# Part of x transposed by the DMA crossbar, and another order of the first half batch, in a fused Sinkhorn attention and bilinear feed-forward kernel

## The chip, the cores and the metric

The kernel runs on one core of a Trainium2 chip. The metric is the device time of one execution in microseconds. Before the change, three runs took 266.49 to 268.1 us, median 268.03 us. A profile is one execution of its own, with a span that leaves out what lies around the program.

## The reference, cut to what matters

Four batches of eight heads, sequence 768 in eight blocks of 96, head dimension 64. Each head has an 8 x 8 matrix P, made doubly stochastic by five Sinkhorn iterations; P mixes the blocks of k and v, and attention runs inside each block. The attention's output, as x of 3072 x 512, goes through a bilinear feed-forward.

```
P = sort_net
for _ in range(5):
    P = exp(P - max(P, -1)); P = P / (sum(P, -1) + 1e-9); P = P / (sum(P, -2) + 1e-9)
k_sorted = einsum('bhij,bhjcd->bhicd', P, k_b)      # the same for v
scores = scale * q_b @ k_sb.T
attn = softmax(scores, -1)
x = (attn @ v_sb) arranged as (4 * 768, 8 * 64)
out = ((x @ w_a) * (x @ w_b)) @ w_out               # 512 -> 1536 -> 512
```

## The kernel before, in words

Work goes by pairs of heads, because two heads of 64 dimensions fill the 128 partitions: 16 pairs, four per batch. For one pair the stages are: q transposed (`stage_q`), k and v mixed with P (`stage_mix`, whose right operand `s_all` is P spread along a diagonal), scores and exponential (`stage_scores`), v transposed back (`stage_v`), the product with v and its normalisation into `xp` (`stage_o`, `one_o`), and x transposed into `xT`, the layout that the feed-forward reads as its moving operand (`to_xT`). `xT` of one batch holds four k-chunks of 128 features, one for each pair; a feed-forward matmul of k-chunk kc reads what pair kc wrote. `to_xT` transposes a pair's 96 x 1024 `xp` as eight 96 x 128 blocks on TensorE into one PSUM tile, which DVE copies to `xT`.

The feed-forward of a batch has 24 steps `ffn_ab` (12 column blocks m of 128, by two halves t of the tokens; each step is four matmuls with `w_a`, four with `w_b`, a copy on ACT and a product on DVE) and six steps `ffn_out` (12 matmuls of 512 columns, a copy to `o_sb`, which has three buffers, and a store from SP's queue).

`interleave` writes the order of TensorE by hand: after each step of one batch's feed-forward come units of attention of the next batch, spread evenly over all steps but the last `spare`. A pair is four units: c (q and the mixes), r (scores and v), o, and x. Batch 1's attention runs beside the second half of batch 0's feed-forward and its outputs (18 steps), that of batches 2 and 3 beside a whole batch's 30 steps. Batch 3's feed-forward has nothing beside it.

Batch 0 is done in two half batches of tokens (four of the eight blocks each), so that the feed-forward can begin early. The first half is one list written out by hand (lines 395 to 451) in `half_q`, `half_mix`, `half_scores`, `half_v`, `half_o` and `half_x`; the order of TensorE, POOL, ACT and DVE follows the list there. `keep_busy` adds matmuls on a zero tile (`fill` of them in a mix, `heat` before it) that compute nothing. `p_rep` repeats each element of P, `to columns` matmuls (line 409) bring it to partitions, and `spread` writes `s_all` from that and a mask: for the first four block rows on DVE, from PSUM; for the second four on POOL, from `p_col`. The list ends with the first nine matmuls of the feed-forward (`begun`: three tiles, k-chunks 0 to 2), and then `half_o(0, 3)` and `half_x(0, 3)`, which give the fourth k-chunk. The second half batch runs as units beside the first half's feed-forward; its first unit is `half_q(1, 0)`.

Loads are issued from POOL's queue in the order written: the first half of batch 0's q, k and v of its four pairs, the weights' column chunks 0 and 1 (`load_ab`, two transfers each), then, after the second `spread`, the second half of q and chunk 2, then chunks 3 to 5 and the later batches. A load waits on POOL when the eighth load before it has not landed.

Of the kernel before, what the change touches and what calls it, by code (L numbers as in the profile page):

```python
# [16 lines left out]
def _ap(t: bass.AP, extra_offset, pattern):  # L17
    return bass.AP(tensor=t.tensor, offset=t.offset + extra_offset,
                   ap=[list(p) for p in pattern])
# [3 lines left out]
def kernel(  # L23
# [11 lines left out]
    nc = tc.nc  # L35
# [44 lines left out]
    def load_q_half(h):  # L80
        nc.gpsimd.dma_start(out=q_first[h * PH:(h + 1) * PH],
                            in_=_ap(q, h * PH * W, [[W, PH], [S * D, H], [1, W]]))
# [19 lines left out]
    def load_ab(c):  # L102
        for w_ap, w_sb in ((moe_w_a, w_a_sb), (moe_w_b, w_b_sb)):
            nc.gpsimd.dma_start(
                out=w_sb[:, :, c * WC:(c + 1) * WC],
                in_=w_ap.rearrange("(kc p) n -> p kc n", p=P)[:, :, c * WC:(c + 1) * WC])
# [39 lines left out]
    def spread(eng, src, h0, n, i0=0, ni=NB):  # L146
        eng.tensor_tensor(
            out=s_all[:, h0:h0 + n, i0:i0 + ni],
            in0=_ap(mask, 0, [[CG, P], [0, n], [0, ni], [1, CG]]),
            in1=_ap(src, i0 * BH + h0, [[NB * BH, P], [1, n], [BH, ni], [0, CG]]),  # L150
            op=ALU.mult)
# [7 lines left out]
    def keep_busy(ps, n, cols=512):  # L159
        for _ in range(n):  # L160
            nc.tensor.matmul(ps[:, 0:cols], lhsT=warm[:, 0:P], rhs=warm[:, 0:cols],  # L161
                             start=True, stop=True)
# [12 lines left out]
             q_ps.rearrange("p c (i t) -> p c i t", i=NBH))  # L175
        st["q", h, hp] = qT

    def half_mix(h, hp, what, eng, fill=0):
        g = h * HP + hp
        src2 = loaded[hp][0 if what == "k" else 1]  # L180
        to = (kTs if what == "k" else vTs)[g % NBUF]
        mix = psF.tile([P, 512], FP32, tag="F", name="mixh")
        keep_busy(mix, fill)
        for c in range(NCH):
            for e in range(2):
                nc.tensor.matmul(  # L186
                    _ap(mix, e * D * 512 + c * CG, [[512, D], [BLK, NBH], [1, CG]]),
                    lhsT=src2[:, e, c * D:(c + 1) * D],
                    rhs=s_all[:, 2 * hp + e, h * NBH:(h + 1) * NBH], start=True, stop=True)
        copy(eng, to[:, 0:HB], mix[:, 0:HB])  # L190
# [29 lines left out]
    def half_x(h, hp, eng):  # L220
        xT, xp = xT_of(0), st["x", h, hp]
        xt_ps = psF.tile([P, NBH, BLK], BF16, tag="F", name="xt_ps")
        for i in range(NBH):
            nc.tensor.matmul(xt_ps[:, i, :], lhsT=xp[:, i],  # L224
                             rhs=ident[0:BLK, 0:BLK], is_transpose=True)
        copy(eng, xT[:, hp, h * HW:(h + 1) * HW].rearrange("p (i t) -> p i t", i=NBH), xt_ps)
# [76 lines left out]

    def to_xT(g):
        xT, xp = xT_of(g // HP), st[g, "xp"]
        xt_ps = psF.tile([P, NB, BLK], BF16, tag="F", name="xt_ps")
        for i in range(NB):
            nc.tensor.matmul(xt_ps[:, i, :], lhsT=xp[:, i],  # L308
                             rhs=ident[0:BLK, 0:BLK], is_transpose=True)
        nc.vector.tensor_copy(out=xT[:, g % HP, :].rearrange("p (i t) -> p i t", i=NB),  # L310
                              in_=xt_ps)


    hTs = {}
# [52 lines left out]
    with tc.manual_schedule(engines={ET.PE, ET.Pool}):  # L367
        with tc.manual_schedule(engines={ET.Activation, ET.DVE}):
            rsum = const.tile([BH, NB], FP32, name="rsum")
            csum = const.tile([BH, NB], FP32, name="csum")  # L370
            p_fin = const.tile([BH, NB * NB], FP32, name="p_fin")
            p_rep = const.tile([BH, NB * NB, CG // 2], FP32, name="p_rep")
            for it in range(5):
                nc.scalar.activation(out=p_nat, in_=p_nat, func=AF.Exp)
                if it == 2:
                    with nc.allow_low_precision("sum of one one and zeros"):
                        nc.vector.reduce_sum(
                            out=mask, in_=_ap(ident, 0, [[P, P], [1, CG], [CG, NB]]),
                            axis=AX.X)
                nc.vector.reduce_sum(out=rsum, in_=p_nat, axis=AX.X)  # L380
                nc.vector.reciprocal(out=rsum, in_=rsum)
                nc.vector.tensor_mul(out=p_nat, in0=p_nat,
                                     in1=_ap(rsum, 0, [[NB, BH], [1, NB], [0, NB]]))
                nc.vector.reduce_sum(out=csum, in_=p_nat.transpose([0, 2, 1]), axis=AX.X)
                nc.vector.reciprocal(out=csum, in_=csum)
                if it < 4:
                    nc.vector.tensor_mul(out=p_nat, in0=p_nat,
                                         in1=_ap(csum, 0, [[NB, BH], [0, NB], [1, NB]]))
                else:
                    nc.vector.tensor_mul(  # L390
                        out=p_fin.bitcast(BF16).rearrange("h (i j u) -> h i j u", i=NB, j=NB),
                        in0=_ap(p_nat, 0, [[NB * NB, BH], [NB, NB], [1, NB], [0, 2]]),
                        in1=_ap(csum, 0, [[NB, BH], [0, NB], [1, NB], [0, 2]]))
                if it == 3:
                    half_q(0, 0, "act")
                    half_q(0, 1, "act")
            half_q(0, 2, "act")
            half_q(0, 3, "act")

            pc_ps = psA.tile([P, NB, BH], FP32, tag="A", name="pc_ps")  # L400
            heat = psA.tile([P, 2, 512], FP32, tag="A", name="heat")
            keep_busy(heat[:, 0], 7)
            NR = NBH * NB
            for hf in range(2):
                nc.vector.tensor_copy(
                    out=p_rep[:, hf * NR:(hf + 1) * NR],
                    in_=_ap(p_fin, hf * NR, [[NB * NB, BH], [1, NR], [0, CG // 2]]))
                for i in range(hf * NBH, (hf + 1) * NBH):
                    nc.tensor.matmul(
                        pc_ps[:, i, :],  # L410
                        lhsT=p_rep[:, i * NB:(i + 1) * NB].bitcast(BF16).rearrange(
                            "h j t -> h (j t)"),
                        rhs=ident[0:BH, 0:BH], start=True, stop=True)
                if hf == 0:
                    spread(nc.vector, pc_ps, 0, 2, 0, NBH)
                    spread(nc.vector, pc_ps, 2, 6, 0, NBH)
            nc.vector.tensor_copy(out=p_col, in_=pc_ps)

            spread(nc.gpsimd, p_col, 0, 8, NBH, NBH)
            load_q_half(1)  # L420
            load_ab(2)

            half_mix(0, 0, "k", "act", fill=4)
            half_mix(0, 0, "v", "dve")
            half_mix(0, 1, "k", "act", fill=1)
            half_scores(0, 0)
            half_v(0, 0)
            half_mix(0, 1, "v", "dve", fill=1)
            half_mix(0, 2, "k", "act", fill=1)
            half_o(0, 0)  # L430
            half_scores(0, 1)
            half_v(0, 1)
            half_mix(0, 2, "v", "act", fill=1)
            half_mix(0, 3, "k", "act", fill=1)
            half_x(0, 0, "dve")
            half_o(0, 1)
            half_scores(0, 2)
            half_v(0, 2)
            half_mix(0, 3, "v", "act", fill=1)
            half_x(0, 1, "dve")  # L440
            half_o(0, 2)
            half_scores(0, 3)
            half_v(0, 3)
            half_x(0, 2, "act")
            begun = []
            for m, w_sb in ((0, w_a_sb), (0, w_b_sb), (1, w_a_sb)):
                pf = psF.tile([P, 512], FP32, tag="F", name="pf")
                ab_mms(pf, w_sb, 0, m, 0, range(KA - 1))
                begun.append(pf)
            half_o(0, 3)  # L450
            half_x(0, 3, "act")


        for c in range(3, 6):
            load_ab(c)
        for hp in range(2):
            load_pair(1, hp)
# [33 lines left out]
        def units_full(b):  # L491
            us = []
            for g in range(b * HP, (b + 1) * HP):
                def c_(g=g):
                    stage_q(g)
                    stage_mix(g, "k", ("act",))
                    stage_mix(g, "v", ("dve", "act"))

                def r_(g=g):
                    stage_scores(g)  # L500
                    stage_v(g)

                us += [c_, r_, lambda g=g: stage_o(g), lambda g=g: to_xT(g)]
            return us

        def interleave(steps, units, spare):
# [56 lines left out]
```

## Time and profile before

| | |
|---|---|
| median of three runs | 268.03 us (266.49 to 268.1) |
| the profiled execution | 267.88 us, span 266.1 us |
| mean granted TensorE clock | 0.993 |
| TensorE busy | 250.3 us, 94% of the span |
| DVE, ACT, POOL busy | 128.4, 102.8, 51.6 us |
| DMA | 20.85 MB in 24571 packets |

A busy share says how long an engine had work in flight; matmuls are pipelined, so a busy TensorE need not be at its peak rate. The granted clock is given as a share of TensorE's full 2.4 GHz; 0.5 is its lower level, 1.2 GHz. The chain that ended last follows the program back from its end, at each step to what released it.

### The profile page before, as it was taken

What the parts mean: (1) busy time and instruction counts of PE and PEld (TensorE: products, weight loads), DVE (VectorE), ACT (ScalarE), POOL (GpSimd) and SP (SyncE); (2) the same over time, 40 slices, a digit from 0 to 9 for tenths busy, and PEclk for the clock granted to TensorE, in tenths of its full rate; (3) what the DMA queues carried; (4) which work ended last, traced back from release to release, by engine and by line L of the source; (5) the groups of instructions that cost most, each with busy time, mean ns of one, the idle gap of its engine ahead of it and who ended that gap; (6) DMA issues with size and microseconds to landing.
All of it is one profiled execution on the core that took longest, in us unless ns stands there. A gap on an engine that the chain in (4) does not pass through costs nothing.

```text
span 266.1 us, 6056 instructions
## 1 busy us (share of the span) xinstructions
PE 250.3 (94%) x2559; PEld 149.9 (56%) x2569; DVE 128.4 (48%) x296; ACT 102.8 (39%) x202; POOL 51.6 (19%) x70
## 2 busy tenths in 40 slices
PE   0698799999999999999999999999999999999994
PEld 0355466666665556666665456666664456666441
DVE  6745346656763425665654236565653124444111
ACT  3245365465444126455461035445360033333100
POOL 8694687774123000000000000000000000000000
PEclk9999799999999999999999999999999999999999
DMA  6999999999565641000001230000001320000132
GB/s 92 197 197 197 197 204 205 200 203 199 83 89 76 134 96 26 2 2 0 2 0 42 83 118 0 2 0 4 0 2 42 118 79 0 2 0 0 42 118 80
DMA packets 24571, 20.85 MB, mean 78 GB/s; under 512 B 1504, under 2 KB 21472, under 8 KB 24544
## 3 DMA queue, kind: packets, MB, share of 16 engines
q0 software_dynamic: 20944, 14.16, 36.3%
q1 hardware_dynamic: 3600, 6.30, 7.2%
q8 instruction: 20, 0.33, 0.5%
q14 instruction: 7, 0.06, 0.1%
HBM read 28.32 MB, written 6.29 MB: 130 GB/s over the span
## 4 chain that ended last, share of the span: by engine, by line
PE 89%; DVE 7%; ACT 1%; issue 1%; DMA 1%; DVEq 0%
PE pf L323 46%; PE po L351 23%; PE mix L265 3%; PE vs_ps L294 2%; PE o_ps L233 2%; PE q_ps L251 2%; PE sc L283 2%; PE mixh L186 2%; PE xt_ps L308 2%; DVE xp L239 1%; PE mixh L161 1%; DVE hT L344 1%; PE vs_ps L210 1%; DVE xph L239 1%; PE xt_ps L224 1%
## 5 line engine op out<-in xcount | busy, mean ns | idle before, releaser
L344 DVE TENSOR_TENSOR hT<-a_sb,pf 128x384 bf16<-128x384 bf16 x96 | 53.1, 553 | 68.6 <-PE pf L323 55.0
L323 PE MATMUL pf<-xT,w_a_sb 128*128 128x384 bf16 x384 | 79.1, 327 | 0.8 <-ACT xT L155 0.8
L323 PE MATMUL pf<-xT,w_b_sb 128*128 128x384 bf16 x384 | 78.9, 328 | 0.0
L343 ACT CAST a_sb<-pf 128x384 bf16<-128x384 f32 x96 | 46.0, 479 | 70.3 <-PE pf L323 48.8
L351 PE MATMUL po<-w_out_sb,hT 128*128 128x512 bf16 x279 | 63.2, 379 | 0.4
L323 PEld LDWEIGHTS <-w_b_sb 128*128 128x128 bf16 x384 | 37.7, 98 | 26.1 <-issue 1.6
L323 PEld LDWEIGHTS <-w_a_sb 128*128 128x128 bf16 x384 | 34.4, 98 | 20.1 <-issue 0.2
L351 PEld LDWEIGHTS <-hT 128*128 128x128 bf16 x288 | 27.6, 98 | 31.7
L157 DVE COPY o_sb<-po 128x512 f32<-128x512 f32 x12 | 8.3, 692 | 36.6 <-PE po L351 32.2
L155 ACT COPY o_sb<-po 128x512 f32<-128x512 f32 x12 | 7.0, 585 | 48.1 <-PE po L351 37.9
L287 ACT ACTIVATE eT<-sc 96x768 bf16<-96x768 f32 x24 | 18.0, 802 | 4.4 <-PE sc L283 4.4
L239 DVE TENSOR_TENSOR xp<-o_ps,rec 96x512 bf16<-96x512 f32 x24 | 15.7, 683 | 0.2
L92 POOL DMA_DIRECT2D k<-in_k_dram x16 | 11.6, 723 | 20.1 <-PE mix L265 17.7
L155 ACT CAST kT<-mix 128x384 bf16<-128x384 f32 x24 | 10.3, 482 | 10.6 <-PE mix L265 10.6
L92 POOL DMA_DIRECT2D v<-in_v_dram x16 | 11.6, 726 | 3.3 <-PE pf L323 1.5
L233 PEld LDWEIGHTS <-eT 96*128 96x128 bf16 x256 | 10.6, 98 | 2.5
L233 PE MATMUL o_ps<-vs,eT 96*128 96x65 bf16 x256 | 11.4, 193 | 0.0
L296 DVE COPY vs<-vs_ps 96x1024 bf16<-96x1024 bf16 x12 | 8.2, 686 | 4.0 <-PE vs_ps L294 3.9
L237 DVE RECIPROCAL rec<-o_ps 96x8 f32<-96x8 f32 x32 | 5.2, 185 | 9.3 <-PE o_ps L233 9.3
L92 POOL DMA_DIRECT2D q<-in_q_dram x12 | 8.6, 720 | 3.6 <-DMA w_out_sb<-in_moe_w_out_dram 1.8
L170 PE MATMUL q_ps<-ident,q_first 64*64 64x64 bf16 x96 | 3.1, 223 | 6.2 <-DMA q_first<-in_q_dram 6.2
L310 DVE COPY xT<-xt_ps 128x768 bf16<-128x768 bf16 x12 | 6.6, 554 | 4.5 <-PE xt_ps L308 4.5
(72 smaller groups left out, 187.7 us busy)
## 6 DMA issues: line engine op xcount, KB each, us to landing
out_dram<-o_sb SPq DMA_DIRECT2D x18, 256.0 KB, 2.0
k<-in_k_dram POOLq DMA_DIRECT2D x16, 192.0 KB, 7.2
v<-in_v_dram POOLq DMA_DIRECT2D x16, 192.0 KB, 7.2
q<-in_q_dram POOLq DMA_DIRECT2D x12, 192.0 KB, 7.5
w_a_sb<-in_moe_w_a_dram POOLq DMA_DIRECT2D x6, 256.0 KB, 9.4
w_b_sb<-in_moe_w_b_dram POOLq DMA_DIRECT2D x6, 256.0 KB, 10.1
w_out_sb<-in_moe_w_out_dram POOLq DMA_DIRECT2D x3, 512.0 KB, 9.9
out_dram<-o_sb SPq DMA_DIRECT2D x12, 128.0 KB, 2.4
```

The costliest lines, as they stand in the source:

```text
L92: nc.gpsimd.dma_start(out=to, in_=_ap(t, (b * H + 2 * hp) * S * D, [[W, P], [S * D, 2], [1, W]]))
L155: nc.scalar.copy(out=out, in_=in_)
L157: nc.vector.tensor_copy(out=out, in_=in_)
L233: nc.tensor.matmul(o_ps[:, e, i * (D + 1):(i + 1) * (D + 1)], lhsT=eT[:, hf, e, i * BLK:i * BLK + P], rhs=vs[:, i0 + i, e, 0:D + 1], start ...
L239: nc.vector.tensor_tensor(out=_ap(xp, i0 * 2 * D, [[nxp * 2 * D, BLK], [D, 2], [2 * D, NBH], [1, D]]), in0=_ap(o_ps, 0, [[1024, BLK], [512 ...
L265: nc.tensor.matmul(mix[e * D:(e + 1) * D, c // 3, c % 3 * P:(c % 3 + 1) * P], lhsT=src2[:, e, c * D:(c + 1) * D], rhs=s_all[:, 2 * g + e], ...
L287: nc.scalar.activation(out=eT[:, hf, :, 0:HB], in_=sc[0:BLK, :, 0:HB], func=AF.Exp, scale=float(scale))
L296: nc.vector.tensor_copy(out=vs[:, :, :, 0:D], in_=vs_ps[0:BLK])
L323: nc.tensor.matmul(pf[:, 0:HW], lhsT=w_sb[:, kc, m * P:(m + 1) * P], rhs=x_cols(b, kc, t), start=(kc == 0), stop=(kc == KA - 1))
L343: nc.scalar.copy(out=a_sb, in_=pf[:, 0:HW])
L344: nc.vector.tensor_mul(out=hT[:, m, t * HW:(t + 1) * HW], in0=a_sb, in1=ab[1][:, 0:HW])
L351: nc.tensor.matmul(po, lhsT=hT[:, m, c * P:(c + 1) * P], rhs=w_out_sb[:, m, :], start=(m == 0), stop=(m == KO - 1))
```

## The change

In the first half batch, `replicate` for the second four block rows moves from DVE to POOL, and their `to_columns` matmuls and copy come after the first mixes; the fills shrink or go; loads of chunk 2, the second half of q, and chunk 3 are issued before the second `spread`; `half_o(0, 3)` comes before the early feed-forward matmuls. For batches 1 to 3, `to_xT` becomes one transposing DMA on SP's queue for each pair, issued in the unit of o, so that a pair has three units.

```
-    def half_mix(h, hp, what, eng, fill=0):
+    def half_mix(h, hp, what, eng, fill=0, cols=512):
...
-        keep_busy(mix, fill)
+        keep_busy(mix, fill, cols)
...
         xT, xp = xT_of(g // HP), st[g, "xp"]
-        xt_ps = psF.tile([P, NB, BLK], BF16, tag="F", name="xt_ps")
-        for i in range(NB):
-            nc.tensor.matmul(xt_ps[:, i, :], lhsT=xp[:, i],
-                             rhs=ident[0:BLK, 0:BLK], is_transpose=True)
-        nc.vector.tensor_copy(out=xT[:, g % HP, :].rearrange("p (i t) -> p i t", i=NB),
-                              in_=xt_ps)
+        nc.sync.dma_start_transpose(
+            out=xT[:, g % HP, :].rearrange("p (i t) -> p i t", i=NB),
+            in_=xp.rearrange("p i e d -> p (i e d)"))
...
-            keep_busy(heat[:, 0], 7)
+            keep_busy(heat[:, 0], 8)
             NR = NBH * NB
-            for hf in range(2):
-                nc.vector.tensor_copy(
+
+            def replicate(eng, hf):
+                eng.tensor_copy(
                     out=p_rep[:, hf * NR:(hf + 1) * NR],
                     in_=_ap(p_fin, hf * NR, [[NB * NB, BH], [1, NR], [0, CG // 2]]))
+
+            def to_columns(hf):
                 for i in range(hf * NBH, (hf + 1) * NBH):
                     nc.tensor.matmul(
...
-                if hf == 0:
-                    spread(nc.vector, pc_ps, 0, 2, 0, NBH)
-                    spread(nc.vector, pc_ps, 2, 6, 0, NBH)
+
+            replicate(nc.vector, 0)
+            replicate(nc.gpsimd, 1)
+            to_columns(0)
+            spread(nc.vector, pc_ps, 0, 2, 0, NBH)
+            spread(nc.vector, pc_ps, 2, 6, 0, NBH)
+            load_ab(2)
+            load_q_half(1)
+            load_ab(3)
+
+            half_mix(0, 0, "k", "act", fill=2, cols=256)
+            half_mix(0, 0, "v", "dve")
+            to_columns(1)
+            half_mix(0, 1, "k", "act")
             nc.vector.tensor_copy(out=p_col, in_=pc_ps)
-
             spread(nc.gpsimd, p_col, 0, 8, NBH, NBH)
-            load_q_half(1)
-            load_ab(2)
-
-            half_mix(0, 0, "k", "act", fill=4)
-            half_mix(0, 0, "v", "dve")
-            half_mix(0, 1, "k", "act", fill=1)
             half_scores(0, 0)
             half_v(0, 0)
-            half_mix(0, 1, "v", "dve", fill=1)
+            half_mix(0, 1, "v", "dve")
             half_mix(0, 2, "k", "act", fill=1)
...
-            half_mix(0, 2, "v", "act", fill=1)
+            half_mix(0, 2, "v", "act")
...
             half_x(0, 2, "act")
+            half_o(0, 3)
             begun = []
             for m, w_sb in ((0, w_a_sb), (0, w_b_sb), (1, w_a_sb)):
...
-            half_o(0, 3)
             half_x(0, 3, "act")
...
-        for c in range(3, 6):
+        for c in range(4, 6):
             load_ab(c)
...
-                us += [c_, r_, lambda g=g: stage_o(g), lambda g=g: to_xT(g)]
+                def o_(g=g):
+                    stage_o(g)
+                    to_xT(g)
+
+                us += [c_, r_, o_]
```

## Rows read from the trace of the kernel before

**Rows 1.** The page: busy us by engine; the chain that ended last, by engine.
```profile
PE 250.3 (94%) x2559; PEld 149.9 (56%) x2569; DVE 128.4 (48%) x296; ACT 102.8 (39%) x202; POOL 51.6 (19%) x70
...
PE 89%; DVE 7%; ACT 1%; issue 1%; DMA 1%; DVEq 0%
```

**Rows 2.** Stretches: length, busy us by engine, granted clock, DMA share, GB/s.
```profile
15.03:24.07 9.04, 8.62 (x186) 5.93 (x186) 5.69 (x14) 5.97 (x10) 6.55 (x9) 1.00 1.42 198
24.07:28.74 4.67, 2.85 (x27) 1.54 (x26) 1.02 (x3) 1.04 (x4) 2.71 (x4) 1.00 1.45 197
28.74:34.65 5.91, 5.60 (x87) 3.27 (x87) 1.65 (x4) 3.15 (x7) 4.64 (x6) 0.71 1.38 198
...
98.00:160.00 62.00, 61.90 (x647) 37.88 (x646) 31.63 (x63) 25.71 (x52) 0.00 (x0) 1.00 0.09 31
```

**Rows 3.** Order of time: start, duration, instruction, idle before it; around x's transposes.
```profile
60.53 0.29 PEld L308 LDWEIGHTS <-xp 96*128 96x128 bf16 x4
...
61.27 0.47 PEld L323 LDWEIGHTS <-w_a_sb 128*128 128x128 bf16 x4
...
69.16 0.28 PEld L308 LDWEIGHTS <-xp 96*128 96x128 bf16 x4
...
107.59 0.52 PEld L308 LDWEIGHTS <-xp 96*128 96x128 bf16 x8
...
108.05 0.47 PEld L323 LDWEIGHTS <-w_a_sb 128*128 128x128 bf16 x4
```

**Rows 4.** The chain that ended last in order of time: a fill; two output steps.
```profile
17.86 0.32 PE mixh L161
...
92.19 5.18 PE po L351 x24
```

**Rows 5.** Order of time: the last o of batch 1.
```profile
88.36 0.76 PEld L233 LDWEIGHTS <-eT 96*128 96x128 bf16 x16
...
90.11 0.69 DVE L239 TENSOR_TENSOR xp<-o_ps,rec 96x512 bf16<-96x512 f32 x1
```

**Rows 6.** The page: DMA queues (packets, MB, share of 16 engines); issues (us to landing).
```profile
q0 software_dynamic: 20944, 14.16, 36.3%
q1 hardware_dynamic: 3600, 6.30, 7.2%
...
out_dram<-o_sb SPq DMA_DIRECT2D x18, 256.0 KB, 2.0
k<-in_k_dram POOLq DMA_DIRECT2D x16, 192.0 KB, 7.2
```

**Rows 7.** Order of time, from the spread of P to the first mix.
```profile
10.80 0.74 POOL L104 DMA_DIRECT2D w_b_sb<-in_moe_w_b_dram  x1 [0.23 <-DMA v<-in_v_dram]
...
12.00 0.75 DVE L147 TENSOR_TENSOR s_all<-mask,pc_ps 128x128 bf16<-128x128 bf16 x2 [0.38 <-PE pc_ps L409]
...
13.21 1.89 PE L161 MATMUL mixh<-warm 128*128 128x512 bf16 x4
...
13.83 1.09 POOL L147 TENSOR_TENSOR s_all<-mask,p_col 128x512 bf16<-128x512 bf16 x1 [2.29 <-DVE p_col L417]
...
15.03 0.53 PE L186 MATMUL mixh<-s_all,k 128*64 128x64 bf16 x12
```

**Rows 8.** Order of time, end of the first half batch.
```profile
26.67 0.69 DVE L239 TENSOR_TENSOR xph<-o_ps,rec 96x512 bf16<-96x512 f32 x1
...
27.42 0.34 PE L224 MATMUL xt_ps<-ident,xph 96*128 96x96 bf16 x4 [1.02 <-DVE xph L239]
...
28.32 0.32 PE L323 MATMUL pf<-xT,w_a_sb 128*128 128x384 bf16 x1 [0.56 <-ACT xT L155]
...
28.74 0.38 PE L170 MATMUL q_ps<-ident,q_first 64*64 64x64 bf16 x12
```

**Rows 9.** Order of time: loads from POOL that waited for earlier loads to land.
```profile
22.91 0.74 POOL L104 DMA_DIRECT2D w_b_sb<-in_moe_w_b_dram  x1 [0.96 <-DMA q_first<-in_q_dram]
...
25.48 0.72 POOL L92 DMA_DIRECT2D v<-in_v_dram  x1 [0.66 <-DMA w_b_sb<-in_moe_w_b_dram]
```

## The prediction

> **What bounds the kernel now.** I read the busy shares and the chain that ended last first: TensorE is busy for 94% of the span and holds 89% of the chain [rows 1]. Next, the same by stage. From 98 to 160 us TensorE is busy for 61.90 of 62.00 us at a granted clock of 1.00, with DVE and ACT near half [rows 2]: there whatever TensorE issues costs its own time, and what leaves its queue is gained in full unless something new arrives late. The start is different. From 24.07 to 28.74 us TensorE works only 2.85 of 4.67 us, and from 28.74 to 34.65 it is busy but the granted clock is 0.71 on average, so much of it runs at the lower level, 1.2 GHz [rows 2]. So I costed the two halves of the change against these two stretches separately. The third view is the DMA's: in each of the stages from 15 to 35 us it moves 197 or 198 GB/s [rows 2], so in that time a transfer lands when the bytes queued ahead of it have landed, not when it was issued.
>
> **Transposes to the crossbar.** Removed: 12 groups of 8 TensorE transposes and 12 DVE copies. I price a group by what TensorE's weight loads show: from the first load of the group to the first load of what follows. In batch 1 that is 61.27 - 60.53 = 0.74 us, 0.3 of it a wait for DVE's xp; in batch 2, 108.05 - 107.59 = 0.46 [rows 3]. Three groups are like the first, nine lie between 0.46 and 0.52 us: 3 x 0.74 + 9 x 0.48 = **6.5 us**, all on the path. The DVE copies (0.55 us each) lay beside TensorE's work and count nothing.
>
> Added: 12 transposing transfers on SP's queue, 96 x 1024 bf16, 192 KB each. The first three of a batch have a whole batch's work ahead of them. The last is read by the next batch's first feed-forward. The interleave places 12 units instead of 16: with 18 steps and 2 spare the last o comes after step 15, with three output steps behind it. Two such steps take 5.18 us of TensorE [rows 4], so three take 7.8 (0.216 us for a matmul of 512 columns, so 0.16 for one of 384). From the first weight load of o until xp is complete: 90.11 + 0.69 - 88.36 = 2.44 us [rows 5]. The fourth k-chunk is read o's 0.76 + 7.8 + 3 x 0.16 us after that load, so the transfer has 9.0 - 2.44, about **6.5 us**, in batch 1. In batches 2 and 3 (30 steps) four output steps follow, and with a DVE copy in the way it has about 8.5 us.
>
> No row shows a crossbar transfer. From below, a 256 KB store from the same SP queue lands in 2.0 us [rows 6]. From above: xp is 768 runs of 256 bytes, 48 for each of 16 engines. q0's packets took 36.3% of 16 x 266.1 us for 20944, 74 ns each; q1's 85 ns [rows 6]. If every run costs a packet, that is 3.5 to 4.1 us, and with the store's 2.0 us about 6. Loads of 192 KB from POOL land in 7.2 us [rows 6], but mostly in the stretches at 198 GB/s; from 98 us the queue carries 31 [rows 2], and the last transpose of batch 1 lies between. I take 5 us, nearer the packet estimate because the runs are short: hidden in all three batches. At 7.2 it would cost 0.7 us once. On SP's queue a store may now stand behind a transpose that still waits for xp and be late by up to 2.4 us; o_sb has three buffers, so the output step 7.8 us later is the first to feel it: no cost.
>
> The Trainium skill, Advanced Engine Details and Errata, section X-Bar Transpose, calls trn2's transposing DMAs as fast as plain ones, 350 to 400 GB/s; by that the sum would be the same, with more slack. No run here shows it yet.
>
> **The start.** Before, the first half of the columns of P reached s_all by 12.75 us (12.00 + 0.75), but the first mix started at 15.03: the queue ran to_columns for the second half and four 512-column fills, 1.89 us, first [rows 7]. After: two fills of 256 columns, at that row's pace some 0.2 us each, from 12.0 on, so the first mix starts at 12.4: **2.6 us** earlier. POOL's copy for the second half begins when its queue has issued the weights ahead of it, 10.80 + 0.74. POOL needed 1.09 us for 512 elements of 2 bytes per partition [rows 7]; this is 256 of 4, so 0.5 to 1.1 us, ended by 12.7. Its columns are wanted after two mixes of 0.5 us, at 13.4, so nothing waits. The extra heat matmul, under 0.5 us, runs in the hole before the spread: nothing. Three later fills go, 0.32 us each [rows 4]; ACT's exponentials and copies are close behind TensorE here (5.97 of 9.04 us [rows 2]), so of 0.96 I take **0.3 us** (bounds 0 and 0.96).
>
> half_o(0, 3) moves ahead of the nine early feed-forward matmuls. Before, the matmuls stood ahead of o, DVE ended xph at 27.36, and TensorE stood for 1.02 us before the last x transposes at 27.42, then 0.56 for ACT's copy [rows 8]. After, the nine matmuls (9 x 0.16, some 1.4 us) cover DVE's 0.69 us and the reciprocal before it: **1.0 us** gained, the 0.56 stays. The o itself must now wait for its exponential, which idle time of before partly contains: bounds 0.4 and 1.4.
>
> Sum: 2.6 + 0.3 + 1.0 = 3.9 us, and half_q(1, 0), at 28.74 before [rows 8], would start at 24.8. **But its data is late.** POOL now issues weights chunk 2, then the second half of q, then chunk 3, ahead of the second spread. Before, the order was spread, q, chunk 2; the waits of POOL's later issues show q landed by 22.91 and chunk 2's second half by 25.48 [rows 9]. The same bytes in another order put q third: near 25.4. So TensorE is held about 0.6 us and the start gives 28.74 - 25.4 = **3.3 us**, not 3.9. The second-half spread moves back by five issues of 0.74 us and what they wait for, from 13.8 to some 16 to 18; its mix is due after 25, so that is free, as is chunk 2, which comes earlier.
>
> **The clock.** The loss from 28.74 to 34.65 is (1 - 0.71) x 5.91 = 1.7 us [rows 2], after a stretch with TensorE 61% busy. After the change the waits left in front (0.56 for ACT, 0.6 for q, those for hT) make a stretch not much denser, so I leave the 1.7 us lost.
>
> **Sum.** The profiled execution took 267.88 us, span 266.1; the median of the runs is 268.03, so no scaling. 267.88 - 6.5 - 3.3 = **258.1**, forecast 258.
>
> **Rivals.**
> *The clock stays up* at 2.4 GHz through that stretch: a further 1.7 us, **256.4**. For it: the 1.02 us hole, the longest, goes. Against: the wait for q takes its place.
> *The start gives nothing* because another wait there (exponentials, a late POOL copy, a colder TensorE without fills) eats it: 267.9 - 6.5 = **261.4**. Against: 2.6 us of it is a queue that only has to be reordered.
> *Transfers somewhat late*, 7 to 9 us each: stalls of 0.5 to 2.5 us in batch 1 and up to 0.5 in each other, **259 to 262**.
> *Transposes slower than the work between them* (the other side). The o units of batch 1 come 7.9 us apart (69.16 - 60.53 between two groups of before [rows 3], less 0.74). If the crossbar lets through only some six of 16 engines' runs at a time, a transfer takes 128 x 74 to 85 ns + 2.0, about 12 us. Then the queue on SP falls behind by 4.1 us twice, wins nothing back in the last gap (one step, three output steps and a pair's other work, 11.8), and the last transpose lands 20.4 us after its xp: 14 us of stall. Batches 2 and 3, with 8.5 us to give, stall 3.5 each: 258.1 + 21 = **279**. It decides from about 10 us a transfer, where the same sum gives 10 us. Against: with all 16 engines it is 6 us at most. For: no row shows that they work side by side here. The Trainium skill, VectorE: DVE Perf Modes, section The three transpose paths, gives the crossbar 1309 ns for 128x128 against TensorE's 390, and its Rules for kernel authors prefer TensorE where PSUM will do; eight blocks one after another would by that, an estimate, be 10.5 us, and the time some 270.
> That the transposes don't leave the path at all, the next batch waiting for each, is this rival in small.
>
> **How the numbers follow.** Forecast 0.42, clock up 0.33, start gives nothing 0.08, somewhat late 0.06, slower 0.11. The range, 254 to 262, takes in the first four, with q landing earlier or a warmer TensorE at the start for up to 2 us below 256.4. One per cent, 2.7 us, is about what a measurement can tell from no change. The first four cases end below 265.3, less a share for what I mis-sized: faster 0.86; of the last, part falls within 1%: same 0.06, slower 0.08.
>
> **What would show it.** First mix near 12.4 and half_q(1, 0) near 25.4, held by the DMA of q_first: right. If it is held by something else, my order of landings is wrong. The granted clock from 25 to 31 us tells forecast from first rival. In the landing times of the transposes, below 6.5 us means hidden; TensorE idle ahead of a batch's first feed-forward means the late cases. No gaps between feed-forward steps where the transposes stood: 6.5 us confirmed. It is wrong if the last transposes are still in flight when their batch begins.

## The result and the profile after

The changed kernel takes 259.4 us (median of four runs, 257.77 to 260.11), the kernel before 267.75; the ratio is 0.9688, interval 0.9631 to 0.9744. Forecast were 258.0 and a range of 254 to 262. The profiled execution is the slowest of the four, 260.11 us with a span of 258.4, so against the one before (267.88 and 266.1) the trace explains 7.7 us. In all that follows, a run that lay over 1.5% above the fastest of its kernel (two of `e5_seven_heats`, one each of `e4_eight_pieces` and `e6_o_late`) is left out of the ratios, though not of the medians.

The page after: busy us by engine, the chain by engine, and the hardware DMA queue (packets, MB, share of 16 engines).

```profile
PE 243.8 (94%) x2469; PEld 145.3 (56%) x2469; DVE 121.4 (47%) x283; ACT 102.7 (40%) x202; POOL 52.0 (20%) x71
...
PE 87%; DMA 7%; POOL 2%; DVE 1%; issue 1%; ACT 0%; POOLq 0%; DVEq 0%
...
q1 hardware_dynamic: 13200, 8.66, 13.8%
```

Against [rows 1] TensorE has 6.5 us less busy time, and in the chain the DMA now holds 7% instead of 1%, 5% of it the load of q. In order of time, the start of the changed kernel:

```profile
12.23 0.38 PE L186 MATMUL mixh<-s_all,k 128*64 128x64 bf16 x12
...
23.23 0.32 PE L320 MATMUL pf<-xT,w_a_sb 128*128 128x384 bf16 x1 [0.56 <-ACT xT L155]
...
26.01 0.38 PE L170 MATMUL q_ps<-ident,q_first 64*64 64x64 bf16 x12 [2.29 <-DMA q_first<-in_q_dram]
```

The first mix starts at 12.23 instead of 15.03 [rows 7], the feed-forward's fourth k-chunk at 23.23 instead of 28.32, 5.1 us earlier [rows 8]. Then TensorE stands for 2.29 us until q lands, and half_q(1, 0) is only 2.7 us earlier than before. Not all of this is the new order: the 12 matmuls of a mix take 0.38 us here and took 0.53 at 15.03 [rows 7], a difference of pace to which the first experiment comes back. Stretches of the changed kernel (length, busy us by engine, granted clock, DMA share, GB/s):

```profile
11.59:23.70 12.11, 10.91 (x216) 7.59 (x216) 7.61 (x19) 6.95 (x13) 7.93 (x11) 1.00 1.41 198
23.71:26.00 2.29, 0.01 (x1) 0.00 (x0) 0.55 (x1) 0.36 (x1) 0.70 (x1) 1.00 1.45 196
26.00:31.70 5.70, 5.58 (x85) 3.27 (x85) 1.18 (x3) 2.58 (x6) 3.52 (x5) 0.70 1.45 196
```

After the hole the granted clock is 0.70 on average for 5.7 us, the same 1.7 us loss as in [rows 2].

For the rest, two c units of batch 1 in weight loads (start, duration), and the last o of batch 1 with its transfer on SP's queue:

```profile
59.09 0.36 PEld L251 LDWEIGHTS <-q 128*64 128x64 bf16 x12 [0.32 <-DMA k<-in_k_dram]
...
67.04 0.36 PEld L251 LDWEIGHTS <-q 128*64 128x64 bf16 x12 [0.32 <-DMA k<-in_k_dram]
...
83.38 0.76 PEld L233 LDWEIGHTS <-eT 96*128 96x128 bf16 x16
...
85.83 1.22 SPq L306 DMA_TRANSPOSE xT<-xp  x1
...
91.66 0.31 PEld L320 LDWEIGHTS <-w_a_sb 128*128 128x128 bf16 x2
```

Pairs come 7.95 us apart, 8.63 before [rows 3]: 0.68 less. The last transpose of batch 1 is issued 2.45 us after its o began, and 2.8 us later it has landed, at 88.6; its reader is due after 92.1. Of the DMA's issues (KB where given, median us to landing):

```profile
out_dram<-o_sb SPq DMA_DIRECT2D x18, 256.0 KB, 2.0
...
xT<-xp SPq DMA_TRANSPOSE x12, 2.8
```

No reader waits: from 60 to 200 us TensorE is busy for 140.0 of 140.0 us. The first two transposes, beside loads at about 200 GB/s, took 9.6 and 8.7 us, the third 4.9; nobody was waiting for those. From the fourth on they took 2.8 to 4.4. Packets of the hardware queue went from 3600 to 13200: 800 for each transfer, that is, its 768 runs of 256 bytes one by one and a few more.

### The profile page after: what moved, and what is told of

Same layout as the page of the kernel before. It is cut to its first block, busy times and chain, and to the rows that moved or that the text cites. A ratio compares the mean times of both kernels' runs of the same rounds, so it can differ in the third digit from the quotient of the medians.

```text
span 258.4 us, 5883 instructions
## 1 busy us (share of the span) xinstructions
PE 243.8 (94%) x2469; PEld 145.3 (56%) x2469; DVE 121.4 (47%) x283; ACT 102.7 (40%) x202; POOL 52.0 (20%) x71
## 3 DMA queue, kind: packets, MB, share of 16 engines
q1 hardware_dynamic: 13200, 8.66, 13.8%
HBM read 28.32 MB, written 6.29 MB: 134 GB/s over the span
## 4 chain that ended last, share of the span: by engine, by line
PE 87%; DMA 7%; POOL 2%; DVE 1%; issue 1%; ACT 0%; POOLq 0%; DVEq 0%
PE pf L320 48%; PE po L348 24%; DMA q_first<-in_q_dram 5%; PE mix L265 3%; PE o_ps L233 3%; PE vs_ps L294 3%; DMA v<-in_v_dram 2%; PE q_ps L251 2%; PE sc L283 2%; PE mixh L186 1%; POOL w_b_sb L104 1%; PE q_ps L170 1%; POOL k L92 1%; PE vs_ps L210 1%; PE sc L198 0%
## 5 line engine op out<-in xcount | busy, mean ns | idle before, releaser
L320 PEld LDWEIGHTS <-w_a_sb 128*128 128x128 bf16 x384 | 35.0, 98 | 21.4 <-issue 0.3
L287 ACT ACTIVATE eT<-sc 96x768 bf16<-96x768 f32 x24 | 18.0, 802 | 5.8 <-PE sc L283 5.8
L170 PEld LDWEIGHTS <-q_first 64*64 64x64 bf16 x96 | 2.5, 135 | 9.5 <-DMA q_first<-in_q_dram 9.0
L202 ACT ACTIVATE eT<-sc 96x768 bf16<-96x768 f32 x8 | 6.5, 807 | 3.6 <-PE sc L198 3.6
```

The source lines that it names most:

```text
L170: nc.tensor.matmul(q_ps[e * D:(e + 1) * D, c, :], lhsT=q_first[rows, 2 * hp + e, c * D:(c + 1) * D], rhs=ident[rows, rows], is_transpose=True)
L287: nc.scalar.activation(out=eT[:, hf, :, 0:HB], in_=sc[0:BLK, :, 0:HB], func=AF.Exp, scale=float(scale))
L320: nc.tensor.matmul(pf[:, 0:HW], lhsT=w_sb[:, kc, m * P:(m + 1) * P], rhs=x_cols(b, kc, t), start=(kc == 0), stop=(kc == KA - 1))
```

## The experiments

**The two parts, alone.** The kernel before with only the new `to_xT` and three units a pair:

```
-        xt_ps = psF.tile([P, NB, BLK], BF16, tag="F", name="xt_ps")
...
+        nc.sync.dma_start_transpose(
+            out=xT[:, g % HP, :].rearrange("p (i t) -> p i t", i=NB),
+            in_=xp.rearrange("p i e d -> p (i e d)"))
...
-                us += [c_, r_, lambda g=g: stage_o(g), lambda g=g: to_xT(g)]
+                us += [c_, r_, o_]
```

> The kernel before with only the transposing DMA for batches 1 to 3. Theory A (a group of transposes costs TensorE what its matmuls take, 0.34 us, plus the wait for xp in three of them): 5.1 us less, ratio 0.981. Theory B (the step of the prediction: 0.46 to 0.74 us a group, 6.5 us less, and the changed kernel lost 1.2 elsewhere): ratio 0.976. Rival (the two parts lean on each other): less than 4 us, ratio above 0.985.

Measured 261.59 us, ratio 0.9802 (0.9772 to 0.9833): 4.5 to 6.1 us less. Theory A's 5.1 lies in the middle, B's 6.5 outside. Why a group is worth 0.34 us shows in the chain of the kernel before, in order of time (start, duration), around one group of batch 2:

```profile
105.31 2.60 PE pf L323 x16
107.91 0.34 PE xt_ps L308 x8
108.25 2.60 PE pf L323 x16
```

In TensorE's own time the eight transposes hold 0.34 us. The 0.46 us between weight loads [rows 3] counts another 0.12 that is not lost: the loads that follow a group come closer together, 0.53 us from a's first to b's first instead of 0.65.

The two profiles settle it, each with one stretch of 3.4 us at a granted clock of 0.50. The last output copy starts 233.65 us after half_q(1, 0) in the kernel before (262.39 - 28.74) and 228.56 us after it here (255.82 - 27.26): 5.1 us less. As a whole these two executions differ by 6.2 us: the 5.1, less 0.4 for a last store that lands later here, and 1.5 in a start that is the same in both kernels:

```profile
13.07 1.04 PE L161 MATMUL mixh<-warm 128*128 128x512 bf16 x4
14.04 0.38 PE L186 MATMUL mixh<-s_all,k 128*64 128x64 bf16 x12
...
27.26 0.38 PE L170 MATMUL q_ps<-ident,q_first 64*64 64x64 bf16 x12
```

Here four fills took 1.04 us, in the profile before 1.89, and the first mix started at 14.04 instead of 15.03 [rows 7]. So the same start can take 1.5 us more or less, and the profile before is the later of the two. The granted clock of [rows 2], 1.00 from 15.03 on, does not show it; the durations do.

And the start alone, the changed kernel with the transposes on TensorE:

> The changed kernel with the transposes of batches 1 to 3 back on TensorE and four units a pair. Theory: only the start gains, 2.7 us, because q holds it at 26.0: ratio 0.990. Rival (the transposing DMAs cost the start something through the DMA queue): more than 3.3 us, ratio under 0.988. Rival (the start's gain is given back later when TensorE has to issue the transposes): under 1.5 us, above 0.994.

Measured 263.49 us, ratio 0.986 (0.9832 to 0.9889), 3.0 to 4.5 us less, somewhat more than the theory said. The rival that blames the transposing DMAs can't be the reason: the first of them is issued at 58 us. Its trace shows q landing for a start at 25.25, not 26.01, and a granted clock of 1.00 after the shorter hole (by their mean clocks, 0.997 and 0.998 against 0.991 to 0.993, in three of the six runs):

```profile
25.25 0.37 PE L170 MATMUL q_ps<-ident,q_first 64*64 64x64 bf16 x12 [1.27 <-DMA q_first<-in_q_dram]
```

Why q lands 0.8 us earlier in one kernel than in the other, with the same loads in the same order, no run settles; in `e8_hole_filled`, with those loads too, it lands at 25.4 (issued at 13.60, 11.8 us to landing). The product of the two ratios, 0.9802 x 0.986 = 0.9665, lies inside the interval of the whole change: the parts add.

**The order of loads.**

```
-            load_ab(2)
             load_q_half(1)
+            load_ab(2)
             load_ab(3)
```

> The changed kernel with one edit: the second half of q is issued ahead of the weights' chunk 2, as before the change. Theory (the order of loads holds TensorE): q lands near 23 to 24 us instead of 26.0, half_q(1, 0) starts near 23.8, 2.2 us sooner, and the time falls by about 2 us against the changed kernel; if the hole of 2.3 us was also what lowers the clock after it, by another 1.7. So 0.955 to 0.962 of the kernel before. Rival (the order does not matter, since the weights' chunks are then late instead, or the queue is full): the wait moves to a feed-forward step and the time stays within 0.5 us of the changed kernel, ratio 0.967 to 0.970.

Measured 256.53 us (256.49 to 256.79), ratio 0.9605 (0.9577 to 0.9633): 2.9 us below the changed kernel's median (2.2 by the two ratios), and the best kernel of the case. half_q(1, 0) starts without a wait for the DMA, and the clock stays up after it (order of time, then a stretch as above):

```profile
23.63 0.38 PE L170 MATMUL q_ps<-ident,q_first 64*64 64x64 bf16 x12
```

```profile
28.00:29.00 1.00, 1.00 (x26) 0.69 (x24) 0.70 (x2) 0.55 (x2) 0.44 (x1) 1.00 1.45 195
```

The weights' chunk 2, now behind q, delays nothing. So the order of two issues, in a stretch where the DMA moves 195 to 198 GB/s throughout, was worth a quarter to a third of the whole change.

**The clock, by itself.** The changed kernel with its own order of loads, and the hole filled with matmuls that compute nothing:

```
+        def first_step():
+            ffn_ab(0, 0, 0, begun[0:2])
+            hole = psA.tile([P, 2, 512], FP32, tag="A", name="hole")
+            keep_busy(hole[:, 0], 10)
```

> The changed kernel, with q as late as there (26.0), and ten matmuls of 512 columns on the zero tile put into the hole of 2.3 us ahead of half_q(1, 0). They compute nothing. Theory (the idle hole is what lowers the clock after it): the granted clock stays at 1.00, half_q(1, 0) still starts near 26.0, and the time falls by the 1.7 us of the dip: 257.7 to 258, ratio 0.963 to 0.965. Rival (the clock falls for another reason, such as the load from the start on): the dip from 28 to 31 us stays and the ratio is 0.968 to 0.971.

Measured 258.26 us (258.15 to 258.51), ratio 0.9676 (0.9652 to 0.9701). In order of time, and the stretch that was at half clock:

```profile
24.04 2.10 PE L161 MATMUL hole<-warm 128*128 128x512 bf16 x9
...
26.07 0.38 PE L170 MATMUL q_ps<-ident,q_first 64*64 64x64 bf16 x12
```

```profile
28.00:29.00 1.00, 0.99 (x38) 0.80 (x31) 0.82 (x2) 0.47 (x3) 0.70 (x1) 1.00 1.45 196
```

half_q(1, 0) is as late as before, held now by the fills (nine of the ten are recorded) and no longer by q, and the clock no longer falls: the idle hole lowers it. The mean clocks of all five runs, 0.996 to 1.00, leave no room for the dip either, which costs 0.007 of a mean. The ratio alone can't tell the two theories apart (the intervals overlap), the trace does: from half_q(1, 0) to the end of the span it is 230.6 us instead of 232.4, 1.8 less. Between medians the gain is 1.1 us. One of the four runs of the changed kernel, 257.77 us at a mean clock of 1.00, had no dip to begin with; by their mean clocks (1.00 in that one, 0.99 in the others) it went as the prediction's first rival, the other three as the forecast. What else parts the medians is not shown, and a mean clock alone does not give the time: the kernel before has runs of 266.3 us at 0.991 and of 267.3 at 0.998.

**The terms of the start**, each taken out of `e1_q_sooner`, where q does not hide them. First the o:

```
             half_x(0, 2, "act")
-            half_o(0, 3)
             begun = []
...
+            half_o(0, 3)
             half_x(0, 3, "act")
```

> e1_q_sooner with half_o(0, 3) after the early feed-forward matmuls again. Theory (the prediction's term): TensorE waits about 1.0 us for the last xph, half_q(1, 0) starts 0.8 to 1.0 later than in e1_q_sooner (23.63), time 257.4, ratio 0.963 to 0.965; with another 1.7 if the longer hole lowers the clock. Rival (o waits for its exponential anyway, so that the order is worth little): under 0.4 us, ratio under 0.962.

Measured 259.73 us, ratio 0.972 (0.9685 to 0.9755): 3.2 us slower, more than any of the theories without the clock. The wait is there again, and half_q(1, 0) comes 1.7 us later, not 1.0:

```profile
24.02 0.34 PE L224 MATMUL xt_ps<-ident,xph 96*128 96x96 bf16 x4 [1.02 <-DVE xph L239]
...
25.35 0.38 PE L170 MATMUL q_ps<-ident,q_first 64*64 64x64 bf16 x12
```

```profile
28.00:29.00 1.00, 1.00 (x22) 0.62 (x22) 0.50 (x2) 0.00 (x0) 0.69 (x1) 0.50 1.45 196
```

The clock falls too, another 1.5 us, though not in every run: two of the six took 258.5 us at mean clocks of 0.999 and 1.00, 2.0 us above `e1_q_sooner`. Between the last two groups of x transposes this kernel takes 3.48 us (20.54 to 24.02) and `e1_q_sooner` 2.04 (20.27 to 22.31), so the order of o is worth 1.4 us; the other 0.3 was lost before it, where the two kernels run the same list. Of the 1.4, 1.02 is the wait that I had counted, and 0.24 one that I had not: with o late, the early matmuls come so soon that the third waits for ACT's copy of the third pair.

```profile
21.45 0.32 PE L320 MATMUL pf<-xT,w_a_sb 128*128 128x384 bf16 x1 [0.24 <-ACT xT L155]
```

Next the order of the mixes:

```
-            half_mix(0, 0, "k", "act", fill=2, cols=256)
-            half_mix(0, 0, "v", "dve")
             to_columns(1)
-            half_mix(0, 1, "k", "act")
             nc.vector.tensor_copy(out=p_col, in_=pc_ps)
+            half_mix(0, 0, "k", "act", fill=4)
+            half_mix(0, 0, "v", "dve")
+            half_mix(0, 1, "k", "act")
```

> e1_q_sooner with the columns of the second half, their copy and four fills of 512 columns ahead of the first mix again. Theory (the prediction's term of 2.6 us, of which the clock is part): the first mix starts at 13.2 if the fills run at full rate and at 14 to 15 at half rate, against 12.2; half_q(1, 0) moves by as much, 1 to 2.6 us, ratio 0.964 to 0.970. Rival (the exponentials and copies of ACT set the pace from there on and absorb it): under 0.5 us.

Measured 258.63 us, ratio 0.968 (0.9651 to 0.9709): 2.1 us slower in the medians. half_q(1, 0) starts at 26.25, 2.6 us after that of `e1_q_sooner`, whose first mix is at 12.31: ACT absorbs nothing of it. But the clock is part of it, as the theory said, and fell right here (order of time, then a stretch as above):

```profile
13.03 1.46 PE L161 MATMUL mixh<-warm 128*128 128x512 bf16 x4
14.42 0.54 PE L186 MATMUL mixh<-s_all,k 128*64 128x64 bf16 x12
...
26.25 0.38 PE L170 MATMUL q_ps<-ident,q_first 64*64 64x64 bf16 x12
```

```profile
14.00:15.00 1.00, 1.00 (x24) 0.58 (x24) 0.00 (x0) 0.01 (x1) 0.56 (x1) 0.50 1.45 195
```

The same order with fast fills has its first mix at 14.04 (`e2_crossbar_alone`), so of the 2.6 us the order is worth about 1.7 and the clock 0.9: 0.4 before the first mix, 0.5 from there to the x transposes of the third pair (8.47 us against 7.96).

Last the extra heat matmul (`keep_busy(heat[:, 0], 8)` back to 7):

> e1_q_sooner (median 256.5, ratio 0.9605) with seven heat matmuls instead of eight. In the changed kernel the mixes ran at full rate from 12.2 us on, before it TensorE was at half rate until about 16. Theory (the eighth heat, which ends 0.4 us before the next matmul instead of 0.8, keeps the rate up): the fills and first mixes are at half rate again, the start loses 0.5 to 1.5 us, ratio 0.963 to 0.966. Rival (the moved mixes, which close the hole from 12 to 13 us, did it): half rate or not, no more than 0.3 us, ratio 0.960 to 0.962.

Measured 256.76 us, ratio 0.9613 (0.9586 to 0.9641): no difference, the rival. The fills and mixes run at the same pace as in `e1_q_sooner`, from 11.85 us on:

```profile
11.85 0.39 PE L161 MATMUL mixh<-warm 128*128 128x256 bf16 x2
```

**Transposes in eight pieces.** The prediction's rival on the other side needed transfers of 10 us or more:

```
-        nc.sync.dma_start_transpose(
-            out=xT[:, g % HP, :].rearrange("p (i t) -> p i t", i=NB),
-            in_=xp.rearrange("p i e d -> p (i e d)"))
+        for i in range(NB):
+            nc.sync.dma_start_transpose(
+                out=xT[:, g % HP, :].rearrange("p (i t) -> p i t", i=NB)[:, i:i + 1],
+                in_=xp[:, i].rearrange("p e d -> p (e d)"))
```

> The changed kernel with each transposing DMA split into eight of 96 x 128. Theory (a transfer is mostly issue and completion, and SP spends 1.2 us on each issue): eight take about 9 to 12 us a pair, the last one of batch 1 lands some 10 us after xp and the next batch waits 3 to 6 us for it, those of batches 2 and 3 up to 3 each: 4 to 10 us above the changed kernel, ratio 0.985 to 1.005. Rival (issue scales with the bytes, so a piece costs an eighth): no change, ratio 0.967 to 0.971. Rival (eight waits for landing one after another, 2.8 us each, 22 us a pair): over 40 us slower.

Measured 279.75 us, ratio 1.0437 (1.0385 to 1.049). The direction of the theory was right, the size was not. SP's queue (in a view that ends before the fourth pair's eighth piece) and TensorE in order of time:

```profile
56.99 32.75 SPq L307 DMA_TRANSPOSE xT<-xp  x24
89.84 3.74 SPq L356 DMA_DIRECT2D out_dram<-o_sb  x6
93.68 8.82 SPq L307 DMA_TRANSPOSE xT<-xp  x7
```

```profile
105.11 0.48 PE L321 MATMUL pf<-xT,w_a_sb 128*128 128x384 bf16 x1 [13.17 <-DMA xT<-xp]
```

The issue of a piece of 24 KB keeps SP for 1.2 us, as that of 192 KB does, so eight make nearly 10 us a pair, pairs come every 7.95 us, and the queue falls behind; three output steps' stores stand in it too, ahead of the fourth pair's pieces. TensorE waits 13.2 us for batch 1's last k-chunk, and the clock is down in and after it (0.64 from 91.3 to 105.1 us, 0.62 from there to 110). The queue on SP that falls behind is the rival's mechanism, and the price is near its 279 us; the cause is another, issues of 10 us a pair and not transfers of 12, since a piece lands in 2.3 us once the loads are done.

## Why the prediction was right, and where its terms were off

*The bound.* TensorE's own time in the steady stages, as read: what left its queue was gained there, and nothing new came late.

*The transposes: 6.5 us predicted, 5.4 measured* (the whole 7.7 us less the 2.7 of the start, plus 0.4 for a last store that lands later after TensorE's end; 5.1 alone, in `e2_crossbar_alone`). The step that was mis-sized is the price of a group: 0.34 us, with the wait for xp 0.68, in place of 0.46 and 0.74. I read it between weight loads, which run ahead of the matmuls and catch up after a short one; the chain of the same trace had the 0.34.

*The transfer: 5 us taken, between 2.0 and 6; 2.8 measured* where it counts, against 6.5 available: hidden with 3.5 us to spare. It came out near the store, at the lower end, though each run is a packet as assumed: (13.8% of 258.4 - 7.2% of 266.1) x 16 engines over 9600 packets is 27 ns each, a third of the 74 and 85 of [rows 6]. The Trainium skill, VectorE: DVE Perf Modes, section The three transpose paths, gives 1.3 us for one block of 128 x 128. Here eight blocks of 96 x 128 took 2.8 in one transfer, and one of them alone 2.3 (`e4_eight_pieces`), so they do not cost eight times one block. The advice of the same page of the Trainium skill, section Rules for kernel authors, to prefer TensorE does not hold here, where TensorE is the bound and the landing is covered. Advanced Engine Details and Errata, section X-Bar Transpose, of the Trainium skill, has them as fast as plain transfers. Here they were somewhat slower, 2.8 us for 192 KB beside 2.0 for a store of 256 KB.

*The start: 3.3 us predicted, 2.7 measured.* The mechanism was the one forecast: TensorE comes early and q holds it. Since q sets what is gained, the whole miss is that q came at 26.0, not 25.4; with these loads it landed at 25.2 and 25.4 in two other kernels, so this is within its spread. There is luck in the size, though: both the forecast and the result count from half_q(1, 0) at 28.74, which came at 27.26 in another execution of the same start. The terms behind TensorE's own time were too small, and that only made the hole longer: 2.3 us where I had 0.6. TensorE was ready 5.0 us earlier, not 3.9. By the two profiles, 2.8 of it comes before the first mix, 0.8 from there to the x transposes of the third pair, and 1.4 from there to those of the fourth (23.93 and 27.42 before, 20.29 and 22.33 after):

- The mixes, 2.6 in the sum, gave 2.8, but only about 1.8 of it is the order (14.04 in `e2_crossbar_alone` less 12.23). The other 1.0 is pace: I took 1.89 us for four fills as their cost [rows 7], where the same fills took 1.04 in another execution.
- From there to the third pair, where I had 0.3 for the fills, it is 0.8, again with some of it pace; no run takes the three fills out alone.
- The o gave 1.4 instead of 1.0: the sum left out the early matmul's wait of 0.24 for ACT; for the last 0.2 there is no row.

*The clock.* The forecast left the 1.7 us lost, and so it was in the profiled execution and, by their mean clocks, in two more of four. The reason given, a wait for q in place of the wait for x, is what the filled hole and the moved load confirm. But it took a hole four times as long as the forecast's 0.6 us: with 1.27 us the profile of `e3_start_alone` shows no dip, nor do, by their mean clocks, two more of its six runs. So the clock came out as forecast in part by luck.

*The sum.* The two terms together were 1.7 us too large, the last store adds 0.4, and so the profiled execution stands 2.0 us above the 258.1 of the sum (the median 1.3).

## What to carry to other kernels

Price what leaves the bounding engine in its matmuls' own time along the chain, not between weight loads, and look at durations as well as at the clock's row: the fills that set the price of the start ran at about half the pace of another execution. When a reordering makes an engine arrive earlier, look at once for the next thing that is due there: on a DMA queue without pauses, two issues swapped cost 2.4 us and, through the idle hole, the clock for up to another 1.7. A transposing transfer is cheap where its reader is a few microseconds away and one issue does the whole pair.

## What the runs showed of the hardware

Issuing a transposing DMA kept SP 1.2 us for 192 KB and for 24 KB alike; it landed in 2.8 us on a quiet queue and in up to 9.6 beside loads at 200 GB/s. In the profiles, TensorE idle for 2.3 us, or for 1.0 with shorter holes near it, was followed by 3.4 us at a granted clock of 0.50; there was none when the hole was filled with matmuls on zeros, and none with a hole of 1.27. Four fills of 512 columns took 1.89 us before [rows 7], 1.46 with the late mixes at the same place, and 1.04 in `e2_crossbar_alone`, whose start is the one of before; so the same code runs there at either pace, the eighth heat matmul is not the reason, and no run here names it.
